# Placing a kernel's zero matmuls by a sliding sum of TensorE work, with stores in threads of their own

## The chip, the cores and the metric

The program runs on one core of a Trainium2 chip. The metric is the device time of the whole program in microseconds (us); lower is better. Five runs of the kernel before are given.

## The reference

Two layers read the same input x (2048 positions by 512 channels, bfloat16) and are mixed by a gate:

```
g = sigmoid((x * gate_w).sum(-1))            # one number per position
q, k, v = split(x @ wqkv)                    # 32 heads of 16 channels
p = softmax(q @ k.T * 16**-0.5)              # 2048 x 2048 for each head
a = (p @ v) @ wo
dt = exp(log_dt); P = exp(dt*(A_re + i A_im) * l)      # l = 0 .. 2047, 128 states per channel
K = sum over states of C * P * dt*B, real part         # 512 x 2048 taps
b = causal_convolution(x, K) + x * Dskip               # the reference does it by FFT
out = g * a + (1 - g) * b
```

The attention needs 32 x 2048 x 2048 exponentials, and nothing else in the program is as large. The convolution is done here by blocks: a table of powers, a state recurrence over 32 chunks of 64 positions, and small matmuls.

## The kernel before, in words

**A program planned ahead.** The Python code runs a planner. Each instruction is an object `O` with an engine, the buffers it reads and writes, a planned cost, and for a matmul a number of `u` units of TensorE work. `Prog.put` appends it to its engine's list, notes a planned end time, and derives the semaphore waits. Engines then run their lists strictly in order. What the planner gets wrong shows up as an engine that stands.

**The backbone.** Scores are made in slots of 128 keys by 512 queries; 2048 slots are grouped three to a tile, 683 tiles in all. For tile t, `fill` issues three score matmuls (operands Qm and KT) into one of two PSUM buffers SC0 and SC1, and `ex` (line 720) issues one ScalarE exponential over all three slots into a ring of SBUF buffers (ET, EX, EL, EM). A fill of tile t+2 must wait for the exponential of tile t. The loop over t at the end of `record` is this backbone.

**Relief for ScalarE.** From a certain tile on, `dchoose` may take one slot of a tile away from ScalarE. VectorE then makes its exponential: one instruction from PSUM (line 732), and for each pair of such slots four instructions into DP and DC (`dpoly`, lines 752, 847, 847, 756). The exponential of that tile covers 1024 columns and not 1536, and the slot's value matmul becomes three matmuls, of which one reads VC, a scaled copy of V made once by `vcopy` (line 795). The tuples `RINGS` and `DWS` say from which tile on which ring is used.

**Everything else is threads.** Value matmuls (`pv`, into PSUM OA), projections, the power table (`table`), the tap stage (`kstage`: Kst, stored to gm_kpd), the state stage (`sstage`: Sst, stored to gm_sd), the recurrence (`scan`), the output stage (`ystage`: Yst, stored to gm_ytd), the gate (64 one-column matmuls) and the output projection are Python generators with priorities; a lower number goes first. Each yields lists of instructions, or a condition: AFTER a mark, Q for a tile number, LOCK for the one spare PSUM bank MB. `Sched.run` picks, for each tile, what is ready by the plan. In the kernel before, a stage yields its own store to DRAM, so its store carries the stage's priority (table 9, kstage 8, ystage 7.5, sstage 7), and loads (`qload`, `sload`, `yload`, `yread`) have 6. All of these DMAs are issued from SyncE's queue (SP) in order. A DMA that transposes (Qt, SG, Yl) holds SP for several us while it is issued.

**Zero matmuls.** `keep` and `keepsc` make a 128x128x512 matmul with an all-zero weight tile `wm`. They add zero to OA, MB or SC and change nothing but TensorE's activity. Where they go is decided by a debt: each tile adds 2.3 units per us of exponential (`WARM`), each matmul pays its units, the debt is cut to between 0 and 4, and after the other work of a tile zero matmuls are added while more than .2 is owed:

```
sch.debt = max(0.0, min(4.0, sch.debt - sch.units)) + WARM * (e1 - e0)
...
while sch.debt - sch.units > .2 and p.free["PE"] + .3 < lim:
```

**Units.** A 128x128x512 matmul is 1 unit; a fill of three is 1; four value matmuls are 1; a gate matmul is set to .05, 3.2 for all 64.

Of the kernel before, what the change touches and what calls it, by code (L numbers as in the profile page):

```python
# [13 lines left out]
P = 128  # L14
# [16 lines left out]
NO = 14  # L31
RINGS = ((24, "ET", NE), (400, "EL", 11), (548, "EM", 14))
DWS = ((400, 548 - 4, "DPL", "DCL", 4, 4.6), (548, 9999, "DPM", "DCM", 7, 5.5))
WARM = 2.3
DEBT = 2.4
SOLO = 1.0
ORDER = """
B161^ zr fo OnTp1^ OnTp0 DPL MU^ Yl gp Py^ wm msk Tt VV D48^ Qp3^ SG2^ EX^ OnT2^ Wo^ ldt tt2^ D32^ DPM Dp hpi^ L8^ g an^ ft1^ PT0^
Dpb^ EM^ X22 ET dt^ nwi^ X23^ EL^ idb Wv Kst u1 u4^ G ea OT BreT^ VE^ pt1^ B160 OnT3 L1^ e2 Qp2^ OnT0 cb^ D16^ Qm L48^ BimT^ x0n^
SG0 PT1^ VC KT^ L16 u2^ ON^ Yst^ Q0 L32^ AreT u3^ Rz^ DCM X20 ge Q1 Q2 SG1 DCL CreT s2^ s3 zi^ FP^ Wk CimT Sst tt1^ pt2 ft2^ Q3  # L40
OnT1^ VL idf L4^ sb_^ X21 Wq gwT Qt bn wrb AimT^ piota^ xT sgn B163 L2 ba^ B162 g1
"""
# [40 lines left out]
class Prog:  # L83
# [4 lines left out]
    def __init__(self, bufs):  # L88
        self.bufs = bufs
        for b in bufs.values():  # L90
            b.st, b.tags, b.closed, b.first, b.last = {}, {}, False, None, None
        self.q = -1
        self.log = []
        self.ops = {e: [] for e in self.ENG}
        self.cnt = {e: 0 for e in self.ENG}
        self.known = {e: {} for e in self.ENG}
        self.snap = {}
        self.dn = [0] * NDSEM
        self.dnext = 0
        self.need = {e: set() for e in self.ENG}  # L100
        self.te = {}
        self.free = {e: 0.0 for e in self.ENG}
        self.aend = 0.0

    def _deps(self, eng, R, W):
# [85 lines left out]
    def put(self, o):  # L191
# [28 lines left out]
        else:  # L220
            self.free[eng] = t + o.c
            e = t + (o.c if o.l is None else o.l)
        self.te[(s, i)] = e
        self._record(eng, o.fn, deps, s, i, o.R, o.W)
        return e

    def emit(self, nc, es):
# [37 lines left out]
class Sched:  # L265


    def __init__(self, prog):
        self.p = prog
        self.thr = []  # L270
        self.flag = set()
        self.lock = {}
        self.n, self.units, self.debt = 0, 0.0, 0.0

# [42 lines left out]
    def emit(self, th):  # L317
        for o in th[3]:
            self.p.put(o)
            if o.eng == "PE":  # L320
                self.units += o.u
        self._next(th)
        self.control()
# [12 lines left out]
    def run(self, now, pe_end, dve_end, margin=.02):  # L336
        p = self.p
        self.control()
        while True:
            best = None  # L340
            holder = [t for t in self.thr if t in self.lock.values()]
            for th in holder + [t for t in self.thr if t not in holder]:
# [8 lines left out]
                if ops[0].dma:  # L351
                    if max(r, f) > pe_end:
                        continue
                    k = 0
                elif eng == "PE":
                    c = sum(o.c for o in ops)
                    if max(f, r) + c > pe_end or self.debt - self.units > DEBT and sum(o.u for o in ops) < 2.3 * c:
                        continue
                    k = 0 if r <= f + .03 else 2
                elif eng == "DVE":  # L360
                    if max(f, r) > dve_end:
                        continue
                    k = 0 if r <= f + .03 else 1 if r <= f + .16 else 2
                else:
                    if r > now:
                        continue
                    k = 0
# [180 lines left out]
def record(p, B, ins):  # L548
# [11 lines left out]
    def mm(out, lhsT, rhs, R, W, start=True, stop=True, pos=None, c=.22, l=.4, u=1.0):  # L560
        kw = {} if pos is None else dict(tile_position=pos)
        return O("PE", lambda t: t.matmul(out(), lhsT(), rhs(), start=start, stop=stop, skip_group_check=True, **kw), R, W, c, l, u)  # L562

    def dv(fn, R, W, n, k=1):
# [227 lines left out]
    def vcopy():  # L792
        yield ("Q", DWS[0][0] - 5)
        yield [dv(lambda v: v.memset(VC(272, [[288, 16], [1, 16]]), 0.0), [], [(VC, 1)], 256)]
        yield [dv(lambda v: v.tensor_scalar(VC(0, [[288, 16], [34, 8], [1, 34]]), VE(34, [[560, 16], [68, 8], [1, 34]]), C3, None, ALU.mult),
                  [(VE, c) for c in range(16)] + [(VE, "one"), (VE, "pad")], [(VC, 0)], 4352, 4)]

    def pv(q):
# [3 lines left out]
        for j in range(4):  # L802
# [8 lines left out]
            if isd:  # L811
# [4 lines left out]
                rounds[1].append(mm(out, ve, lambda DP=DP, o=o: DP(o, [[1, 512]]), rv + [(DP, k, g["n"])], [(OA, 0, b)], False, False, **kw))  # L816
                rounds[2].append(mm(out, vc, lambda DC=DC, o=o: DC(o, [[1, 512]]), [(VC, 0), (VC, 1), (DC, k, g["n"])], [(OA, 0, b)], False, kt == 15, **kw))
        os = [o for r in rounds for o in r]
# [174 lines left out]
    def table():  # L993
# [5 lines left out]
        for pb in range(NBLK // 2):  # L999
            qr, blks = pb // 2, (2 * pb, 2 * pb + 1)  # L1000
            PT = PTs[pb % 2]
            if pb > 1:
                yield ("AFTER", f"K{2 * pb - 3}")
            B16 = B[f"B16{qr}"]
# [17 lines left out]
            for i, blk in enumerate(blks):  # L1022
                yield [dma("SP", lambda e, i=i, blk=blk, PT=PT: e.dma_start(ptd.dram(blk * P * PTN, [[PTN, P], [1, PTN]]), PT(i * PTN, [[1, PTN]])),
                           [W[i]], [(ptd, blk)], 6.5, .5)]
                sch.mark(f"pt{blk}")
                if blk == 15:
                    sch.mark("sgfree")
                sch.add(qload(blk), 6)
                sch.add(kstage(blk), 8)

    X2 = [B[f"X2{k}"] for k in range(4)]
# [9 lines left out]
    def kstage(blk):  # L1041
# [4 lines left out]
        for part, wn in ((0, "wrb"), (1, "nwi")):  # L1046
# [7 lines left out]
        sch.unlock("MB")  # L1054
        yield [dma("SP", lambda e: e.dma_start(kpd.dram(blk * P * 8 * P, [[8 * P, P], [1, 8 * P]]), Kst(1024 * (blk % 2), [[1, 8 * P]])),
                   [(Kst, blk % 2, blk), (Kst, "z")], [(kpd, blk)], 4.5, .4)]
        sch.mark(f"K{blk}")
# [3 lines left out]
    def sstage(blk):  # L1061
        q0, qr, bl = (blk % 2) * PTN, blk // 4, blk % 4
        for bank in range(4):
            yield ("LOCK", "MB", [(Qt, blk % 2, blk)])
            os = []
            for pp in range(2):
                for j in range(4):
# [9 lines left out]
            sch.unlock("MB")  # L1077
            yield [dma("SP", lambda e, bank=bank: e.dma_start(sd.dram((CB * blk + 8 * bank) * 8192, [[256, P], [4 * 8192, 2], [1, 256]]),
                                                              Sst(512 * bank, [[256, 2], [1, 256]])), [(Sst, bank, (blk, bank))],
                       [(sd, (blk, bank))], 2.7, .45)]  # L1080
        sch.mark(f"S{blk}")
# [75 lines left out]
    def ystage():  # L1157
        def unit(u):
# [11 lines left out]
            for qq in range(2):  # L1170
# [9 lines left out]
                for q in (2 * qq, 2 * qq + 1):  # L1180
                    for ri in range(2):
# [9 lines left out]
            sch.unlock("MB")  # L1191
            yield [dma("SP", lambda e: e.dma_start(ytd.dram(16 * u * S, [[T, P], [4 * S, 4], [1, T]]), Yst(r2 * 256, [[64, 4], [1, 64]])),
                       [(Yst, r2, u)], [(ytd, u)], 3.3, .65)]
            if hf == 1:
# [208 lines left out]
    def pvs(t, limit):  # L1403
        nonlocal pvn, opened
        done_ = 0
        while pvn < NQ and done_ < 2:
# [39 lines left out]
            put(*os)  # L1446
            sch.units += sum(o.u for o in os)
            sch.mark(("pv", pvn))
# [10 lines left out]
    while tile(t + 1):  # L1459
# [4 lines left out]
        e1 = e0 + (512 * len(acols(t + 1)) / 1200 + EXP if tile(t + 1) else 0)  # L1464
        sch.debt = max(0.0, min(4.0, sch.debt - sch.units)) + WARM * (e1 - e0)
        sch.units = 0.0
        sch.control()
        if tile(t + 2):
# [13 lines left out]
            put(*fill(t + 2))  # L1482
            sch.units += 1
            if t + 2 in dsel:
# [11 lines left out]
        pvs(t, lim)  # L1496
        while sch.debt - sch.units > .2 and p.free["PE"] + .3 < lim:
            if opened:
# [11 lines left out]
            put(o)  # L1510
            sch.units += 1
    p.late, p.forced = late, forced[0]
# [58 lines left out]
```

## Time and profile before

| | |
|---|---|
| median of 5 runs | 895.15 us (890.76 to 898.02) |
| the profiled execution | 897.99 us |
| its span on the core | 896.2 us |
| mean granted TensorE clock | 0.965 |
| busy: ScalarE, VectorE, TensorE | 866.1, 826.6, 786.8 us |
| exponentials of 1536 columns | 532 (382 ET, 18 EX, 76 EL, 56 EM) |
| exponentials of 1024 columns | 151 (72 EL, 79 EM) |
| zero matmuls | 579 (531 into OA, 46 into SC, 2 into MB) |
| DMA, mean over the span | 108 GB/s |

The page lists busy time by engine; PE is TensorE's matmuls, PEld its weight loads, DVE VectorE, ACT ScalarE, POOL GpSimdE, and SP the queue from which SyncE issues DMAs. PEclk is the clock that TensorE was granted: 1.00 is full. A name with "SC<-Qm,KT" is a matmul that writes SC and reads Qm and KT. Times inside the span start at its first instruction.

### The profile page before, as it was taken

Reading aid. Unit: us, or ns where it says so; the run is one execution under the profiler, and the core shown is the slowest. Engines: PE = TensorE matmul, PEld = TensorE weight load, DVE = VectorE, ACT = ScalarE, POOL = GpSimd, SP = SyncE. Lnnn points to the kernel's source line nnn. Section 1 sums busy time; section 2 is a strip of 40 time slices with the busy share of each in tenths; the row PEclk is TensorE's granted clock in tenths of the full one; section 3 lists DMA queues with packets and bytes.
Section 4 is the critical chain, followed back from the end, with each engine's and each line's share of the span. In section 5 each row is a group of like instructions: output and inputs, shape, how many; then the busy total and the mean of one; then the engine's idle time right before and its main releaser. Section 6 shows DMA issues by size and latency. Waiting matters only on the chain.

```text
span 896.2 us, 18273 instructions
## 1 busy us (share of the span) xinstructions
PE 786.8 (88%) x7487; PEld 246.9 (28%) x7487; DVE 826.6 (92%) x1769; ACT 866.1 (97%) x693; POOL 9.0 (1%) x18
## 2 busy tenths in 40 slices
PE   7999999888888888888888999998899989898987
PEld 2222232222222222222233333342233322222222
DVE  7999999999867899999999987799999999999992
ACT  6999999999998999999999999799999999999996
POOL 2000000000000000000000000000000000000000
PEclk9999997999997999999999799599999999999999
DMA  9400010006797989969499688566214101000000
GB/s 205 119 1 1 1 49 0 1 1 174 230 217 226 263 283 252 197 136 187 88 206 169 172 185 164 143 141 136 76 41 119 22 19 35 20 1 1 2 1 24
DMA packets 228562, 96.48 MB, mean 108 GB/s; under 512 B 192000, under 2 KB 215168, under 8 KB 226432
## 3 DMA queue, kind: packets, MB, share of 16 engines
q1 hardware_dynamic: 227280, 94.54, 44.0%
q8 instruction: 59, 0.97, 0.5%
q10 hardware_dynamic: 1200, 0.79, 0.3%
q14 instruction: 23, 0.19, 0.1%
HBM read 30.02 MB, written 37.75 MB: 76 GB/s over the span
## 4 chain that ended last, share of the span: by engine, by line
ACT 42%; DVE 41%; PE 12%; issue 2%; DMA 2%; POOL 1%; DVEq 0%; ACTq 0%; SPq 0%; POOLq 0%
ACT ET L720 31%; DVE s L847 9%; ACT EM L720 5%; PE OA L562 5%; PE SC L562 4%; DVE EL L732 4%; DVE DCM L847 4%; DVE DCL L847 3%; ACT EL L720 3%; DVE EM L732 3%; DVE G L847 3%; PE MB L562 3%; ACT EX L720 3%; DVE Sst L1075 2%; DVE SG L1117 2%
## 5 line engine op out<-in xcount | busy, mean ns | idle before, releaser
L720 ACT ACTIVATE ET<-SC 128x1536 bf16<-128x1536 f32 x382 | 516.3, 1601 | 8.6 <-PE SC L562 8.3
L562 PE MATMUL SC<-Qm,KT 32*128 32x512 bf16 x2048 | 274.6, 395 | 82.9 <-ACT ET L720 48.3
L562 PE MATMUL OA<-wm 128*128 128x512 bf16 x531 | 180.6, 404 | 2.8 <-DVE OT L835 1.6
L720 ACT ACTIVATE EL<-SC 128x1536 bf16<-128x1536 f32 (+1 forms) x148 | 169.9, 1305 | 4.8 <-PE SC L562 4.1
L562 PEld LDWEIGHTS SC<-Qm,KT 32*128 32x128 bf16 x2048 | 67.8, 91 | 332.1 <-ACT ET L720 172.4
L720 ACT ACTIVATE EM<-SC 128x1024 bf16<-128x1024 f32 (+1 forms) x135 | 148.8, 1254 | 0.8 <-PE OA L562 0.4
L562 PE MATMUL OA<-ET,VE 128*32 128x512 bf16 x1146 | 117.6, 404 | 0.0
L847 DVE TENSOR_TENSOR s<-G,MU 128x256 f32<-128x256 f32 x240 | 92.5, 420 | 3.4
L847 DVE TENSOR_TENSOR tt<-B,D 128x1024 bf16<-128x1024 bf16 x96 | 62.7, 682 | 0.5
L562 PEld LDWEIGHTS OA<-wm 128*128 128x128 bf16 x531 | 39.0, 99 | 85.9 <-issue 76.1
L1075 DVE TENSOR_TENSOR Sst<-MB,sgn 128x512 bf16<-128x512 f32 x64 | 43.6, 681 | 13.1 <-PE MB L562 13.0
L732 DVE TENSOR_SCALAR EM<-SC 128x512 int16<-128x512 f32 x78 | 51.8, 677 | 0.0
L847 DVE TENSOR_TENSOR s<-s,SG 128x256 f32<-128x256 f32 x120 | 50.0, 417 | 0.0
L847 DVE TENSOR_TENSOR G<-s,s 128x256 f32<-128x256 f32 x120 | 49.8, 415 | 0.1
L732 DVE TENSOR_SCALAR EL<-SC 128x512 int16<-128x512 f32 x72 | 47.9, 679 | 0.5 <-PE SC L562 0.5
L562 PEld LDWEIGHTS OA<-ET,VE 128*32 128x32 bf16 x1146 | 29.2, 94 | 67.3 <-issue 65.9
L562 PE MATMUL OA<-EL,VE 128*32 128x512 bf16 x444 | 44.9, 399 | 0.6 <-DVE OT L835 0.6
L562 PE MATMUL OA<-EM,VE 128*32 128x512 bf16 x404 | 39.6, 388 | 0.1
L835 DVE STREAM_TRANSPOSE OT<-OA 128x512 f32<-128x512 f32 x32 | 22.7, 708 | 17.6 <-PE OA L562 17.6
L562 PE MATMUL MB<-Qt,X 64*32 64x256 bf16 x512 | 29.7, 308 | 10.0 <-DVE Sst L1075 7.8
L847 DVE TENSOR_TENSOR ft<-FP,L 128x1024 f32<-128x1024 f32 (+1 forms) x32 | 33.8, 1086 | 0.4
L1117 DVE CAST SG<-G 128x256 bf16<-128x256 f32 x120 | 34.1, 284 | 0.1
(163 smaller groups left out, 837.6 us busy)
## 6 DMA issues: line engine op xcount, KB each, us to landing
gm_ptd<-PT SPq DMA_DIRECT2D x16, 1024.0 KB, 6.2
Py<-gm_ptd SPq DMA_DIRECT2D x32, 512.0 KB, 4.6
gm_sd<-Sst SPq DMA_DIRECT2D x64, 128.0 KB, 2.6
gm_kpd<-Kst SPq DMA_DIRECT2D x16, 256.0 KB, 4.0
Tt<-gm_kpd SPq DMA_DIRECT2D x128, 32.0 KB, 3.7
gm_xrd<-in_A_x_dram SPq DMA_DIRECT2D x1, 2048.0 KB, 11.0
X<-gm_xrd SPq DMA_DIRECT2D x8, 256.0 KB, 5.0
gm_ytd<-Yst SPq DMA_DIRECT2D x32, 64.0 KB, 2.3
```

Of the source, the lines that this page charges most:

```text
L562: return O("PE", lambda t: t.matmul(out(), lhsT(), rhs(), start=start, stop=stop, skip_group_check=True, **kw), R, W, c, l, u)
L720: return ac(lambda a: a.activation(b(o, F), sc(0, F), AF.Exp, scale=LN2 / 128), [(sc, n, (t, n)) for n in ns], [et(t, n)[2] for n in ns], ...
L732: yield [dv(lambda v: v.tensor_scalar(b(o, [[1, 512]]).bitcast(I16), sc(512 * n, [[1, 512]]), -EOFF, EOFF, ALU.max, ALU.add), [(sc, n, (t, ...
L835: yield [dv(lambda v: v.transpose(OT(0, [[1, 512]]), OA(0, [[1, 512]])), [(OA, 0, b)], [(OT, 0, b)], 560)]
L847: return dv(lambda v: v.tensor_tensor(o(), a(), b_(), f), R, W, n, k)
L1075: yield [dv(lambda v, bank=bank: v.tensor_tensor(Sst(512 * bank, [[256, 2], [1, 256]]), MB(0, [[256, 2], [1, 256]]), sgn(0, [[0, 2], [1, 2 ...
L1117: return dv(lambda v: v.tensor_copy(sg(2 * RS * r, [[RS, 2], [1, 128]]), G(256 * (r % 2), V2)), [(G, r % 2)], [(sg, bl, (qr, 'G')) for bl ...
```

## The change

Four things change together.

1. The debt is gone. The planner keeps a history of TensorE's planned work, and `lack(t)` sums the units of the last 3.413 us before t. Zero matmuls are added while that sum is under 7.6 units, or the last half window under 3.34; other matmul groups are admitted only if the sum does not fall too far behind.
2. The stores of table, kstage, sstage and ystage (16, 16, 64 and 32 of them) become threads of their own with priority 5.9, just ahead of the loads. The stage goes on at once. The table's reuse of a PT buffer now names the taps and stores of both blocks of that buffer.
3. The scaled copy of V is made by four instructions, each for four key tiles, and a value matmul that needs VC reads only its own quarter.
4. Rings and relief windows start a little earlier (tile 380 and 540 for 400 and 548), and the SBUF places of the buffers (`ORDER`) are new.

```diff
-RINGS = ((24, "ET", NE), (400, "EL", 11), (548, "EM", 14))
-DWS = ((400, 548 - 4, "DPL", "DCL", 4, 4.6), (548, 9999, "DPM", "DCM", 7, 5.5))
-WARM = 2.3
-DEBT = 2.4
+RINGS = ((24, "ET", NE), (380, "EL", 11), (540, "EM", 14))
+DWS = ((380, 540 - 4, "DPL", "DCL", 4, 4.6), (540, 9999, "DPM", "DCM", 7, 5.5))
+NEED = 7.6
+WIN = 3.413
+HALF = .44
+TOL = .2
...
+        if eng == "PE":
+            self.hist.append((self.free[eng], o.u))
...
+    def lack(self, t):
+        v, u, h = 0.0, 0.0, NEED * HALF
+        for e, w in reversed(self.hist):
+            if e <= t - WIN:
+                break
+            if e > t - WIN / 2:
+                h -= w
+            u += w
+        return max(NEED - u, h)
...
-                    if max(f, r) + c > pe_end or self.debt - self.units > DEBT and sum(o.u for o in ops) < 2.3 * c:
+                    at = max(f, r) + c
+                    if at > pe_end or now < 1e8 and p.lack(pe_end) - sum(o.u for o in ops) > TOL + max(0, int((pe_end - at) / .24)):
                         continue
...
+    def spawn(op, pr, name=None):
+        def g():
+            yield [op]
+            if name:
+                sch.mark(name)
+        sch.add(g(), pr)
...
-        yield [dv(lambda v: v.tensor_scalar(VC(0, [[288, 16], [34, 8], [1, 34]]), VE(34, [[560, 16], [68, 8], [1, 34]]), C3, None, ALU.mult),
-                  [(VE, c) for c in range(16)] + [(VE, "one"), (VE, "pad")], [(VC, 0)], 4352, 4)]
+        for k in range(0, 16, 4):
+            yield [dv(lambda v, k=k: v.tensor_scalar(VC(288 * k, [[288, 4], [34, 8], [1, 34]]), VE(34 + 560 * k, [[560, 4], [68, 8], [1, 34]]),
+                                                     C3, None, ALU.mult),
+                      [(VE, c) for c in range(k, k + 4)] + [(VE, "one"), (VE, "pad")], [(VC, ("c", k // 4))], 1088, 4)]
...
-                yield ("AFTER", f"K{2 * pb - 3}")
+                for n in ("K", "pt"):
+                    for k in (4, 3):
+                        yield ("AFTER", f"{n}{2 * pb - k}")
...
-            yield [dma("SP", lambda e, bank=bank: e.dma_start(sd.dram((CB * blk + 8 * bank) * 8192, [[256, P], [4 * 8192, 2], [1, 256]]),
-                                                              Sst(512 * bank, [[256, 2], [1, 256]])), [(Sst, bank, (blk, bank))],
-                       [(sd, (blk, bank))], 2.7, .45)]
+            spawn(dma("SP", lambda e, bank=bank: e.dma_start(sd.dram((CB * blk + 8 * bank) * 8192, [[256, P], [4 * 8192, 2], [1, 256]]),
+                                                             Sst(512 * bank, [[256, 2], [1, 256]])), [(Sst, bank, (blk, bank))],
+                      [(sd, (blk, bank))], 2.7, .45), 5.9)
...
-        while sch.debt - sch.units > .2 and p.free["PE"] + .3 < lim:
+        while p.lack(lim) > 0 and p.free["PE"] + .3 < lim:
```

The other three stores change as the one of Sst does, and the remaining lines of the debt are removed.

## The prediction

> **What bounds the kernel now.** I read the engine totals and the clock row of the page first.
>
> ```profile
> PE 786.8 (88%) x7487; PEld 246.9 (28%) x7487; DVE 826.6 (92%) x1769; ACT 866.1 (97%) x693; POOL 9.0 (1%) x18
> ...
> PEclk9999997999997999999999799599999999999999
> ```
>
> ScalarE (ACT) is the bound, and five dents in the clock row (slices of 22.4 us) say where it may lose time. In the list of exponentials the distance from one end to the next has a median of 1.343 us for 1536 columns and 0.917 us for 1024. So the profiled time splits up: first tile done 15.83, then 531 x 1.343 + 151 x 0.917 = 851.6, distances longer than those medians 20.06, last exponential to the span's end 8.70, outside the span 1.80; sum 897.99 us. Only the 851.6 and the 20.06 can move.
>
> Next, the busy time by stretch. The clock record puts the half-clock stretches at 130.4 to 144.0, 277.1 to 287.4, 372.7 to 376.1, 495.6 to 505.8 and 557.0 to 580.9: 13.65, 10.24, 3.41, 10.24 and 23.89 us, or 4, 3, 1, 3 and 7 times 3.413 us. Here are those stretches, each after the 3.4 us ahead of it:
>
> ```profile
> core 0: us, PE busy (x) PEld busy (x) DVE busy (x) ACT busy (x) POOL busy (x), PEclk, DMA share, GB/s
> 126.90:130.40 3.50, 3.06 (x51) 1.45 (x48) 3.50 (x8) 3.50 (x4) 0.00 (x0) 0.99 0.00 0
> 130.40:144.00 13.60, 13.44 (x76) 3.04 (x76) 12.72 (x23) 11.77 (x11) 0.00 (x0) 0.50 0.00 1
> 273.70:277.10 3.40, 2.05 (x17) 0.51 (x16) 1.41 (x4) 3.40 (x4) 0.00 (x0) 1.00 1.03 413
> 277.10:287.40 10.30, 10.13 (x61) 2.29 (x61) 9.34 (x18) 8.10 (x6) 0.00 (x0) 0.50 0.46 170
> 369.30:372.70 3.40, 2.05 (x28) 0.83 (x27) 3.37 (x10) 3.40 (x4) 0.00 (x0) 1.00 1.11 298
> 492.20:495.60 3.40, 2.61 (x66) 1.54 (x62) 3.37 (x11) 3.40 (x4) 0.00 (x0) 1.00 0.89 268
> 553.60:557.00 3.40, 2.10 (x47) 1.06 (x46) 3.37 (x12) 3.40 (x3) 0.00 (x0) 1.00 0.71 150
> 557.00:580.90 23.90, 23.90 (x285) 7.79 (x284) 18.49 (x54) 18.25 (x14) 0.00 (x0) 0.50 0.59 140
> ```
>
> See in it: ACT, full ahead of each stretch, falls to 18.25 of 23.90 inside it. Of the 20.06 us, 15.8 lie in the five stretches (2.5, 2.9, 0.8, 2.6, 7.0) and 4.2 elsewhere. I then weighed each matmul by the array it uses (rows x columns x streamed columns over 128 x 128 x 512) and summed by 3.413 us windows in step with the clock record: the windows just ahead of the five stretches hold 4.56, 5.50, 4.50, 4.75 and 3.50 units, and the lowest full-clock window that nothing follows holds 5.12. So a weak window of about 5 units costs clock. Why they are weak, the waits say:
>
> ```profile
> PE MB L562 <- DVE Sst L1075: 11.0, 20, 1.3
> ACT ET L720 <- PE SC L562: 8.3, 17, 0.9
> PE MB L562 <- DVE Yst L1190: 2.8, 4, 1.3
> ```
>
> In four of the five TensorE stood in order for up to 1.3 us on the MB bank; the first (126.9) holds the gate's one-column matmuls, which the plan counts at 3.2 units and which weigh 0.125.
>
> **Zero matmuls.** By the instruction order they go from 579 to 625: 46 more, x 0.21 us (two take 0.61, three 0.82) = 9.7 us of TensorE, which had 109 us free. In a tile with a full MB they can push a fill and so ACT; I take 0, bound 1 us, since ACT's whole wait for fills at full clock was part of the 4.2. What they buy is where they stand. I laid both programs' matmuls along their exponentials at 1.343 and 0.917 us: the time in which the last 3.413 us hold under 5.0 units falls from 9.4 to 1.6 us, under 5.5 from 23.9 to 14.8. Between tiles 85 and 450 (120 to 620 us) nothing under 5.0 is left, where it was 8.5 us; after 620 us it grows from 0.9 to 1.6. Five episodes scaled by 1.6/9.4 are 0.85, by 14.8/23.9 are 3.1; as the windows that fired lay at 3.5 to 5.5, I take 2. At 15.8/5 = 3.2 us each that leaves 6.4 of 15.8: gain 9.4, bounds 5.9 and 13.1.
>
> A row against this: those windows had PE busy for 2.05 to 3.06 us of 3.4, its longest wait was 1.30 us, and the clock still fell. The Trainium skill, "TensorE: Matmul & The Clock Gate", section "HAM oscillation", has as its rule that idle gaps over some 3.4 us are what costs clock. By that rule no zero matmul was needed and this part gains 0 (894.6 in the sum below); this trace disagrees. The same page (section "What's actually happening") wants one busy window for full clock again, while 557.0 to 580.9 was busy for 23.90 of 23.90 us and stayed at half for seven.
>
> **Relief moved.** The order shows 524 exponentials of 1536 and 159 of 1024 (before 532 and 151): 523 x 1.343 + 159 x 0.917 = 848.2, a gain of 3.4 us on the path. For it VectorE gets 8 x (0.68 + half of 0.41 + 0.68 + 0.68 + 0.41) = 14.2 us more, and TensorE 16 more value matmuls (0.1 us or less each in their column groups). Cover for the 14.2: VectorE stands for 18.9 us between 224 and 314 and 13.2 between 515 and 582, but is full late:
>
> ```profile
> 224.00:314.00 90.00, 75.50 (x673) 21.45 (x677) 71.09 (x131) 87.59 (x66) 0.00 (x0) 0.94 0.90 234
> 515.00:582.40 67.40, 63.28 (x885) 24.54 (x881) 54.16 (x159) 61.75 (x46) 0.00 (x0) 0.82 0.76 164
> 604.80:873.60 268.80, 243.52 (x2285) 74.47 (x2289) 267.29 (x547) 267.31 (x246) 0.00 (x0) 1.00 0.16 39
> ```
>
> So the eight cost nothing if earlier work of VectorE moves up into the 32 us, and up to 14.2 if not.
>
> **Stores.** SP issues 390 DMAs in both. A transposing load of Qt holds SP for 5.4 us (median); a store ready at the same moment now passes it, and the load is 0.45 us later. The trace shows what a late store does: at 275.7 VectorE ended a 2.51 us wait of the Kst cast for an earlier gm_kpd store, and TensorE then stood 1.07 us on MB, which opened the second episode. In the changed order the last Sst comes at tile 312 and not 376, the last recurrence step at 409 and not 427, the last Yst at 495 and not 521: at some 0.68 us or less per instruction this is work that leaves the late, full part of VectorE, so the 14.2 are covered. The mark that the table now awaits adds no instruction; queued behind it are a block pair's 14 VectorE instructions (9 us), whose stores gate Qt. I take 0 for this part alone, bounds -2 (the 2.5 us wait gone) and +3 (two such waits anew).
>
> **V's copy.** One instruction of 1.23 us becomes four; the nearest row (128 x 1024, 16-bit, 0.42 us) gives 1.7: 0.5 us more VectorE at tile 375, 0 on the path. New SBUF places: 10 more waits on VectorE, 4 on TensorE, of some 1,100 each: 0.
>
> **Sum.** 897.99 - 3.4 - 9.4 = 885.2 for the profiled execution. It lies 2.84 above the median, about one episode; scaling the median's loss in the same ratio (15.8 - 2.84 = 13.0, of which two fifths stay) gives 895.15 - 3.4 - 7.8 = 884.0. I say 884. With no episode it is 878.8, and 877 if 1.8 of the 4.2 go too.
>
> **Rivals.** First, the episodes come back: four of five began with an in-order wait that the plan did not foresee, and VectorE is planned fuller between tiles 120 and 240, so waits on MB can be as many. For it: the 20 waits for Sst. Against it: a stand of 1.3 us takes about 3 units, and there is now more around it. Time 890 to 894.6 (897.99 - 3.4). Second, slower: the transfers jam. DMA share was 0.85 between 201.6 and 320 and 0.78 to 440. The same ptd, kpd, Qt and sd traffic ran over tiles 141 to 376 and now over 141 to 312; 0.82 x 235/171 = 1.13. If 1 were the ceiling, 0.13 x 171 x 1.343 = 30 us of delay would fall on 16 blocks, 1.9 us each, on TensorE in front of its Qt matmuls; stands of 1.05 and 1.30 us cost ACT 0.72 and 0.85, so 0.65 x 30 = 20 us: 897.99 - 3.4 + 20 = 914, half of it 904. It decides from the point where Qt lands later than the plan's 12 us; it landed in 7.6 to 9.9. Against it: single 6.4 us stretches show shares of 1.2. Third, the eight slots find VectorE full: 885.2 + 14.2 = 899 at most.
>
> **How the numbers follow.** Forecast 0.64 (877 to 889); episodes back 0.22 (889 to 896, a third of it under 890.7); VectorE full 0.05 (892 to 899); jam 0.09 (over 900). The measurement can tell about 0.5% from no change: 890.7 to 899.6. Faster 0.64 + 0.07 and a little of the rest = 0.73, same 0.18, slower 0.09. The range 877 to 895 leaves out the jam, the worst of the third, and the lowest edge.
>
> **What would show it.** Exponentials 524 and 159, distances 1.343 and 0.917; two half-clock stretches or fewer between 120 and 620 us, the likeliest near 130 us (the gate) or after 800; ACT's distance loss 10 to 11 us for 20.06; VectorE's idle time between 224 and 314 under 10 us; last Yst before 700 us. Wrong, if five stretches are there again, if Qt lands after 12 us, or if waits of ACT for line 732's tiles appear late.

## The result and the profile after

The changed kernel takes 902.37 us (median of 23 runs, 897.3 to 908.7), the kernel before 894.9 us (44 runs, 888.87 to 902.18). The ratio is 1.008, interval 1.0057 to 1.0103: slower, where 884.0 and faster were forecast. (Runs of either kernel spread by 1.3 to 1.5%. The profiled one of the kernel after, 898.45 us, lies low in its spread and the one of before, 897.99 us, high, so the two profiles differ by less than the medians.)

The engine totals and the clock row of the page, after:

```profile
PE 786.0 (88%) x7549; PEld 247.8 (28%) x7549; DVE 839.1 (94%) x1796; ACT 860.9 (96%) x693; POOL 9.2 (1%) x18
...
PEclk9999999999997899999999999999999999999999
```

ScalarE (ACT) has 5 us less work, of which eight wide exponentials turned narrow explain 8 x (1.343 - 0.917) = 3.4, and still the span is not shorter. The clock row has one dip, in the slices from 269 to 314 us, where before it had four spread over the kernel (slices from 134, 269, 493 and 560 us; the fifth half-clock stretch, 3.41 us at 372.7, is too short to show there). The clock record gives six half-clock stretches between 120 and 620 us, at 273.0, 286.6, 317.3, 351.5, 450.5 and 525.6 us, 34.1 us in all (before 61.4). Split up as in the prediction, the profiled execution is: first tile done 14.18, nominal distances 848.2 (524 exponentials of 1536 columns, 159 of 1024), distances longer than nominal 25.58, then 8.70 and 1.80. Of the 25.58 us, 19.7 lie between 245 and 400 us, where before there were 3.8.

Busy time by stretch, after: first the two longest half-clock stretches, then two of the stretches that the prediction used.

```profile
core 0: us, PE busy (x) PEld busy (x) DVE busy (x) ACT busy (x) POOL busy (x), PEclk, DMA share, GB/s
273.00:279.80 6.80, 6.77 (x44) 1.56 (x44) 6.11 (x12) 4.18 (x3) 0.00 (x0) 0.50 1.14 251
286.60:300.30 13.70, 7.85 (x52) 1.58 (x55) 6.79 (x12) 5.84 (x5) 0.00 (x0) 0.50 0.98 278
...
224.00:314.00 90.00, 70.14 (x649) 20.68 (x645) 73.76 (x132) 76.56 (x58) 0.00 (x0) 0.89 0.99 256
...
604.80:873.60 268.80, 236.75 (x2210) 71.08 (x2207) 264.32 (x534) 267.92 (x247) 0.00 (x0) 1.00 0.13 33
```

Between 286.6 and 300.3 TensorE, VectorE and ScalarE are all half idle: they wait for something that is none of them. Over 224 to 314 ScalarE has 76.56 us of work where it had 87.59, and the DMA share is 0.99 where it was 0.90. After 604.8 ScalarE is busy for 267.92 of 268.80 us. The waits, after:

```profile
PEld MB L576 <- DVE Sst L1099: 28.4, 29, 6.4
...
PE MB L576 <- DVE Sst L1099: 21.9, 20, 5.8
...
ACT ET L741 <- PE SC L576: 20.2, 17, 6.1
...
DVE Sst L1099 <- DMA gm_sd<-Sst: 15.7, 6, 5.9
```

(Sum in us, number, longest.) The last row is new (the waits of before have none of Sst for a store): VectorE, about to write an Sst slot, waits for the store that empties it. The timeline around the longest of these waits shows the whole chain (start, length, engine and line, tile; in brackets the idle time ahead and what ended it; SPq is SyncE's queue):

```profile
284.45 1.05 SPq L1048 DMA_DIRECT2D gm_ptd<-PT  x2
...
285.55 2.44 SPq L1102 DMA_DIRECT2D gm_sd<-Sst  x2
...
288.03 7.50 SPq L1061 DMA_TRANSPOSE Qt<-gm_ptd  x1
292.78 0.69 DVE L1099 TENSOR_TENSOR Sst<-MB,sgn 128x512 bf16<-128x512 f32 x1 [5.87 <-DMA gm_sd<-Sst]
...
293.53 0.65 PE L576 MATMUL MB<-Qt,X 64*32 64x256 bf16 x8 [5.85 <-DVE Sst L1099]
...
294.77 1.45 ACT L741 ACTIVATE ET<-SC 128x1536 bf16<-128x1536 f32 x1 [6.14 <-PE SC L576]
```

Two 1 MB stores of the table go out, then two 128 KB stores of Sst. By the DMA records the four land at 289.01, 291.65, 292.76 and 293.40: the small ones need 7.2 and 6.7 us, where the plan allows 2.7. VectorE stands 5.87 us in front of the Sst write, TensorE 5.85 us in front of the next MB matmul, and since the score matmuls are queued behind that, ScalarE stands 6.14 us.

### The profile page after: what moved, and what is told of

The parts are those of the page before. It is cut to its first block, busy times and chain, and to the rows that moved or that the text cites. A ratio compares the mean times of both kernels' runs of the same rounds, so it can differ in the third digit from the quotient of the medians.

```text
span 896.7 us, 18426 instructions
## 1 busy us (share of the span) xinstructions
PE 786.0 (88%) x7549; PEld 247.8 (28%) x7549; DVE 839.1 (94%) x1796; ACT 860.9 (96%) x693; POOL 9.2 (1%) x18
## 4 chain that ended last, share of the span: by engine, by line
DVE 52%; ACT 37%; DMA 5%; PE 3%; issue 3%; SPq 0%; ACTq 0%; DVEq 0%
ACT ET L741 13%; ACT EL L741 13%; DVE s L870 9%; ACT EM L741 8%; DVE tt L870 4%; DVE Sst L1099 4%; DMA gm_sd<-Sst 4%; DVE EM L753 3%; DVE G L870 3%; DVE DCM L870 3%; DVE ft L870 3%; ACT EX L741 3%; DVE EL L753 3%; DVE DCL L870 3%; DVE PT L870 2%
## 5 line engine op out<-in xcount | busy, mean ns | idle before, releaser
L741 ACT ACTIVATE ET<-SC 128x1536 bf16<-128x1536 f32 x362 | 489.4, 1624 | 20.6 <-PE SC L576 20.2
L576 PE MATMUL SC<-Qm,KT 32*128 32x512 bf16 x2048 | 270.5, 389 | 70.0 <-ACT ET L741 23.4
L576 PE MATMUL OA<-wm 128*128 128x512 bf16 x582 | 185.8, 394 | 3.1 <-DVE OT L858 2.0
L741 ACT ACTIVATE EL<-SC 128x1536 bf16<-128x1536 f32 (+1 forms) x160 | 184.8, 1366 | 0.1
L741 ACT ACTIVATE EM<-SC 128x1024 bf16<-128x1024 f32 (+1 forms) x143 | 155.9, 1268 | 0.8 <-PE SC L576 0.5
L576 PE MATMUL OA<-ET,VE 128*32 128x512 bf16 x1086 | 109.8, 399 | 0.4 <-DVE OT L858 0.4
L1099 DVE TENSOR_TENSOR Sst<-MB,sgn 128x512 bf16<-128x512 f32 x64 | 43.6, 681 | 16.6 <-DMA gm_sd<-Sst 15.7
L753 DVE TENSOR_SCALAR EM<-SC 128x512 int16<-128x512 f32 x86 | 56.8, 679 | 0.1
L576 PE MATMUL OA<-EL,VE 128*32 128x512 bf16 x480 | 47.2, 389 | 0.2 <-DVE OT L858 0.2
L576 PE MATMUL OA<-EM,VE 128*32 128x512 bf16 x428 | 41.6, 388 | 0.1
```

The lines of the kernel that those rows point to most:

```text
L741: return ac(lambda a: a.activation(b(o, F), sc(0, F), AF.Exp, scale=LN2 / 128), [(sc, n, (t, n)) for n in ns], [et(t, n)[2] for n in ns], ...
L753: yield [dv(lambda v: v.tensor_scalar(b(o, [[1, 512]]).bitcast(I16), sc(512 * n, [[1, 512]]), -EOFF, EOFF, ALU.max, ALU.add), [(sc, n, (t, ...
L1099: yield [dv(lambda v, bank=bank: v.tensor_tensor(Sst(512 * bank, [[256, 2], [1, 256]]), MB(0, [[256, 2], [1, 256]]), sgn(0, [[0, 2], [1, 2 ...
```

## The experiments

The letters in the expectations stand for theories. A and B in e1 and e2 are explained there; from e3 on, A: Sst has too few slots. C: the DMA engines are over-full. D: SyncE's queue is. E: the order of the instructions is bad in itself. F: a late small store costs only where its slot is written again. G: the wait moves on. Any other is explained where it stands. "Loss" is the sum of the distances over nominal, as above. Each ratio is to the kernel before on the same chip. A kernel that is planned anew also gets SBUF places of its own; e5, e9 and e13 keep those of the changed kernel, e10 those of e1.

**The parts.** e1 is the kernel before with `lack`, its calls and no debt. e2 is the kernel before with the four `spawn` stores and the table's marks.

```diff
 # e1, and the other lines of the debt
-        while sch.debt - sch.units > .2 and p.free["PE"] + .3 < lim:
+        while p.lack(lim) > 0 and p.free["PE"] + .3 < lim:
 # e2, and the same for gm_ptd, gm_kpd, gm_ytd
-            yield [dma("SP", ... sd.dram(...), 2.7, .45)]
+            spawn(dma("SP", ... sd.dram(...), 2.7, .45), 5.9)
```

> The kernel before with the new placing of zero matmuls alone (682 of them for 579; stores, V copy and rings as before). Theory A (the stores, issued earlier, press the transfers and Sst waits for them): last Sst stays at tile 375, no jam between 250 and 320 us, fewer half-clock stretches (3 or fewer), exponentials' distance loss 20 falls to about 10 us; the plan relieves 144 slots for 151, +3 us; time 5 to 8 us under the kernel before, about 888. Theory B (the admission rule and the extra zero matmuls hold up the fills): slower than before by 4 to 8 us, as the whole change is.

> The kernel before with the stores in threads of their own alone (debt, V copy, rings as before). Theory A: last Sst at tile 307, DMA share about 1.06 between 250 and 320 us, Sst waits for gm_sd for 10 us or more, exponentials lose 12 us or more between 250 and 320 us; total 6 to 12 us over the kernel before. Theory B: the stores cost nothing; time within 0.5% of before or 3 us under it (158 slots relieved for 151).

e1: 885.37 us (881.64 to 890.28), ratio 0.9896 (0.986 to 0.9932). e2: 909.15 us (904.4 to 912.99), ratio 1.0164 (1.0122 to 1.0206). The stores alone make the kernel slower than before, in e2 by 15 us and not the 6 to 12 expected; the long wait there is that of Kst for gm_kpd (up to 9.5 us), while Sst waited for gm_sd for 2.3 us in all and not for 10. In e1 the loss is 3.5 us, with no half-clock stretch before the end, and ScalarE never stands where the changed kernel does (busy time by stretch, e1):

```profile
245.00:270.00 25.00, 21.56 (x192) 6.16 (x191) 15.33 (x30) 25.00 (x20) 0.00 (x0) 1.00 1.04 207
270.00:295.00 25.00, 21.38 (x198) 6.33 (x198) 21.27 (x40) 25.00 (x20) 0.00 (x0) 1.00 0.98 288
295.00:320.00 25.00, 21.44 (x207) 6.73 (x211) 24.90 (x49) 25.00 (x20) 0.00 (x0) 1.00 0.90 236
```

e7 adds V's copy in four to e1. e8 adds only the gm_ptd stores, e14 only the gm_kpd stores, e15 all four kinds; e15 is the changed kernel without the ring borders and V's copy:

```diff
 # e8, on e1 (e14: the same for gm_kpd<-Kst)
-                yield [dma("SP", ... ptd.dram(blk * P * PTN, ...)]
-                sch.mark(f"pt{blk}")
+                spawn(dma("SP", ... ptd.dram(blk * P * PTN, ...), 5.9, f"pt{blk}")
```

> The new rule for zero matmuls alone (the kernel of 885.4 us in the first series) with V's scaled copy in four parts added, and nothing else. The prediction took this part at 0: 883 to 888 us. If the four parts cost three more VectorE instructions' overhead on a critical place, or the order that follows is worse, over 890.

> The new rule for zero matmuls alone, and of the stores only the 16 gm_ptd ones queued apart from their stage; the 64 gm_sd, 16 gm_kpd and 32 gm_ytd stores stay in their stages. The state stage keeps nearly its pace (first, middle and last Sst block at tiles 158, 250 and 371; in the changed kernel 158, 234 and 312; with the zero-matmul rule alone 158, 262 and 375). Theories C and D both: what jams is the denser state stage, not stores queued apart as such, so 883 to 889 us. If any store queued apart brings the jam, by reaching SyncE in another order: over 893.

> The zero-matmul rule, and of the stores only the 16 gm_kpd ones queued apart. First, middle and last Sst block at tiles 158, 260 and 380, as with the rule alone (158, 262, 375). If what costs is the denser state stage: 882 to 888 us, loss under 8. If any store queued apart costs, by being planned nearer to the next write of its slot: 890 or more, with a wait of Kst on gm_kpd of over 3 us.

> The changed kernel without the new ring borders (400 and 548 again) and without V's copy in four parts: the zero-matmul rule and all four kinds of stores queued apart. The state stage runs at the changed kernel's pace (158, 234, 312). If the stores alone make the loss: 898 to 906 us, loss 20 or more, waits on gm_sd or gm_kpd or Qt over 5 us. If the ring borders or V's copy have a share: under 894.

e7: 887.86 us, ratio 0.9883 (0.9837 to 0.9929), not to be told from e1: V's copy costs nothing that this measurement can show. e14: 887.82, 0.9952 (0.9927 to 0.9978). It lost nothing between 245 and 400 us, and no wait of Kst on gm_kpd appeared; but its whole loss was 11.2 us and not under 8, of which 3.6 us lie near 140 and 3.7 between 420 and 460 us, in and behind half-clock stretches at 130.0, 423.6 and 440.7. e8: 894.06, 0.9974 (0.9946 to 1.0002), with 9.7 us lost between 245 and 400: just on the side of the second expectation. Its first half did not keep the pace that was expected, though: the 33rd Sst write came after 93 tiles, where e1 has 106. e15: 901.71, 1.0111 (1.0071 to 1.0152), its loss 28.9 and its wait for gm_sd up to 5.8: the ring borders and V's copy have no visible share.

**More slots, and a later landing in the plan.** e3 gives Sst eight slots at the same instruction order; e4 tells the planner that a gm_sd store lands after 8.0 us.

```diff
 # e3; slot bank becomes slot 4 * (blk % 2) + bank
-    sb("Sst", 4 * 512)
+    sb("Sst", 8 * 512)
 # e4
-                      [(sd, (blk, bank))], 2.7, .45), 5.9)
+                      [(sd, (blk, bank))], 8.0, .45), 5.9)
```

> The changed kernel with eight Sst slots for four, so that a slot's next write comes a whole block later; same instructions in the same order on every engine. Theory A (Sst waits for its own store's landing, and VectorE, MB, TensorE and ScalarE stand behind it): the wait of Sst for gm_sd goes from 15.7 us to under 2, the loss of the exponentials between 250 and 320 us from 17 to under 6, time about 885 to 888. Theory C (the DMA engines themselves are full, the wait only moves on): another wait (Qt, Kst or PT for a DMA) takes its place, loss in that stretch stays over 12 us, time 898 or more.

> The changed kernel, but the plan is told that a gm_sd store lands after 8.0 us and not 2.7 (the longest of the trace was 8.0); four slots as in the changed kernel. Theory A: the plan puts Sst where its slot is free, so VectorE does other work meanwhile; wait of Sst for gm_sd under 4 us, time 886 to 890, with the transfers as dense as in the changed kernel (last Sst at tile 302). Theory C: the jam stays, 898 or more.

e3: 904.66 us, ratio 1.0114 (1.0079 to 1.0148). e4: 900.66, 1.0075 (1.0046 to 1.0104). Theory A falls. In e4 Sst still waits for gm_sd (8.1 us in three waits, where under 4 was expected). In e3 that wait is gone and others are there (waits of e3):

```profile
DVE Kst L1075 <- DMA gm_kpd<-Kst: 8.4, 1, 8.4
PE MB L577 <- DMA Qt<-gm_ptd: 8.4, 4, 3.2
```

**Another queue.** e5 issues the gm_sd and gm_kpd stores from GpSimd's queue, e13 the gm_ptd stores; everything else keeps its order:

```diff
 # e5 (e13: ('ptd',))
+        for _, o in log:
+            if o.dma and o.W[0][0].name in ('sd', 'kpd'):
+                o.eng = "POOL"
```

> The changed kernel with the instruction order of TensorE, ScalarE and VectorE untouched, but with the gm_sd and gm_kpd stores (64 and 16 of them) issued on GpSimd's queue, so that they no longer stand behind the Qt transposing loads, which hold SyncE for 5.7 to 6.1 us each. Theory D (the issue queue of SyncE is over-full between 245 and 320 us: SyncE was issuing for 180 of the 220 us between 200 and 420 in the changed kernel, 148 in the one before): the waits 'DVE Sst <- DMA gm_sd<-Sst' (15.7 us) and 'DVE Kst <- DMA gm_kpd' vanish or fall under 3 us, the loss of the exponentials falls from 25.6 to under 10 us, and the time is 881 to 889. Theory C (the 16 DMA engines themselves are full: share 1.06 in that stretch): the stores land as late as before, the waits stay over 8 us, and the time stays at 897 to 905.

> The changed kernel with the instruction order of TensorE, ScalarE and VectorE untouched, and the 16 gm_ptd stores of 1 MB issued on GpSimd's queue instead of SyncE's; the small stores stay on SyncE's. In the changed kernel 22 of 80 gm_sd and gm_kpd stores landed after more than 5 us, 17 of them issued within 5 us behind a gm_ptd store of the same queue. If it is the order of the queue: hardly any of them lands after 5 us, no wait on gm_sd or gm_kpd over 2 us, loss under 14 us instead of 25.6, 882 to 890 us. If it is the DMA engines themselves, shared by all queues: 15 or more still land after 5 us, and Qt, whose load must wait for gm_ptd, lands later too, 895 to 906 us.

e5: 900.9 us, ratio 1.0049 (1.0016 to 1.0083). e13: 913.08, 1.0224 (1.0186 to 1.0262). Both miss what a pure queue theory asks, and e13 is slower than either of its expectations. (In both, 2.5 and 1.7 us come from the end, where 11.17 and 10.40 us follow the last exponential and not 8.70.) In e5 no wait on gm_sd or gm_kpd is left, but Qt lands after 10.5 us (median) and up to 17.0, and TensorE stands for it. Timeline of e5; the Qt loads now hold SyncE for up to 12.0 us each:

```profile
286.54 17.09 SPq L1070 DMA_TRANSPOSE Qt<-gm_ptd  x2
...
302.55 0.65 PE L585 MATMUL MB<-Qt,X 64*32 64x256 bf16 x8 [4.25 <-DMA Qt<-gm_ptd]
```

In e13, 15 of 80 small stores, alone with the loads on SyncE's queue, still landed after more than 5 us, Qt took up to 13.9, and Sst waited as before (waits of e13):

```profile
DVE Sst L1108 <- DMA gm_sd<-Sst: 14.7, 8, 3.9
```

So what is short seems to lie behind the queues. Not shown is how much GpSimd's queue adds of its own (its gm_sd stores landed after 5.1 us in the median, 3.5 in the changed kernel); no run issued the stores from a third queue. By the Trainium skill ("DMA: Bandwidth & Descriptors", section "Issuing engines are not separate DMA queues"), transfers share the same 16 DMA engines, whichever engine issues them. The 15 late stores of e13 agree with it.

**Less and more traffic at the same order.** e9 leaves out the transposition of Qt (so a part of the state computation): the load is then 128 packets of 8 KB and not 4096 of 256 B. e10 is e1 plus 64 useless stores from GpSimd's queue; in the trace they went as packets of 6 KB at 292 ns, 1.17 us of the 16 engines each.

```diff
 # e9
-e.dma_start_transpose(Qt((blk % 2) * PTN, [[128, 32], [1, 128]]), ptd.dram(...))
+e.dma_start(Qt((blk % 2) * PTN, [[1, PTN]]), ptd.dram(...))
 # e10, after each gm_sd store
+prog.put(O("POOL", lambda e, k=k: e.dma_start(X.dram(k * P * 1536, [[1536, P], [1, 1536]]), VE(0, [[1, 1536]])), ...
```

> The changed kernel with its instruction order kept on every engine, but the 16 Qt loads read 8 KB rows as they lie and leave out the transposition (so this kernel leaves out a part of the state computation: Qt holds the table untransposed). In the profile of the changed kernel a block's Qt load is 4096 packets of 256 B at 21.6 ns, that is 5.5 us of all 16 DMA engines; as 128 packets of 8 KB at 324 ns it is 2.6 us. Theory C (the 16 DMA engines are over-full: a block's transfers take about 13.4 us of them and the changed kernel plans a block in 10.0 tiles of 1.343, that is 13.4 us): the waits on gm_sd, gm_kpd and Qt vanish, the exponentials lose under 8 us instead of 25.6, 876 to 886 us. Theory E (not the volume, but the places in which state work now stands before score matmuls): the loss stays over 15, 888 to 900 us.

> The kernel with the zero-matmul rule alone (885.4 us in the first series, loss 3.5 us) with its order kept on every engine, plus 64 useless stores from GpSimd's queue, one after each gm_sd store has landed: 128 rows of 3 KB of a tile that is not written any more, to memory of their own. By the rows between 2 and 4 KB (84 and about 170 ns a packet) one takes about 1.0 us of the 16 DMA engines, a block's four 4 us. Its blocks are then about as full as those of the changed kernel (13.4 + 4 of 17.6 us, against 13.4 of 13.4). Nothing is added to SyncE. Theory C: Qt loads hold SyncE longer than 6.5 us on average and land late, the loss rises to 8 to 25 us, 889 to 905. Theory E, and a pure queue theory: no wait is added, 882 to 888 us.

e10: 930.18 us, ratio 1.0408 (1.0363 to 1.0453): traffic alone turns the fastest kernel into the slowest, more than expected, with no instruction of TensorE, VectorE, ScalarE or SyncE moved. Qt took 12.2 us (median) and up to 20.6. Waits of e10:

```profile
ACT ET L754 <- PE SC L589: 33.7, 23, 6.3
...
DVE Sst L1109 <- DMA gm_sd<-Sst: 13.3, 4, 6.8
...
DVE G L1148 <- DMA SG<-gm_sd: 8.8, 3, 5.6
...
PE MB L589 <- DMA Qt<-gm_ptd: 7.3, 2, 4.1
```

e9: 893.09, ratio 0.9998 (0.9961 to 1.0035); the loss fell from 25.6 to 15.5, not to under 8, and both figures lie in the range that its expectation gave to E. Small stores were late as often as in the changed kernel (27 of 80 after more than 5 us, there 22), and 5.6 us of the loss follow one wait for gm_sd that ends at 287 us (waits of e9):

```profile
DVE Sst L1099 <- DMA gm_sd<-Sst: 7.9, 2, 5.8
```

So fewer packets took away 10 us and left the rest. Against E as the whole cause stands e10, where nothing but traffic was added and the loss rose from 3.5 to 46.2. C held in direction in both, and in size in neither.

**The pace.** e6 raises the planner's figures for SyncE's transfers. e11 keeps them and adds one condition to `qload`; e12 is e11 with eight Sst and four Kst slots; e16 and e17 are e11 with other numbers.

```diff
 # e11, in qload, under `if blk >= 2:`
+            yield ("Q", 144 + 13 * blk)
 # e16 (e17: 9 for 12)
+            yield ("Q", 144 + 15 * min(blk, 7) + 12 * max(0, blk - 7))
 # e6: Qt holds 6.3, SG 7.0/3.2, gm_kpd 5.5/.8, and
-                      [(sd, (blk, bank))], 2.7, .45), 5.9)
+                      [(sd, (blk, bank))], 4.5, .85), 5.9)
```

> The changed kernel with the planner's figures for SyncE raised to what the trace measures: a Qt load holds the queue 6.3 us (was 5.6), an SG load 3.2 (2.6), a gm_sd store .85 (.45) and lands after 4.5 (2.7), a gm_kpd store .8 (.4) and lands after 5.5 (4.5). The planner then slows the state stage by itself: the middle Sst block comes at tile 242 instead of 234. Theory D (the queue of SyncE): SyncE's share of issuing between 245 and 320 us falls below .9, the loss falls under 12 us, 884 to 891 us. Theory C (the DMA engines): the traffic is nearly as dense, share 1.0 or over, so the waits go to Qt and SG landings, and the time is 893 to 901.

> The whole change, all stores still queued apart, with one line more: the Qt load of block b is not planned before tile 144 + 13 b, so that a block has 13 tiles (17.5 us) as in the kernel before, instead of 10. First, middle and last Sst at tiles 158, 250 and 354 (changed kernel 158, 234, 312). Theory C: share of the DMA engines between 245 and 320 us under 1.0, Qt lands within 11 us, no wait on gm_sd or gm_kpd over 2 us, loss under 8 us, 880 to 888 us. Theory E: the loss stays over 15 us, 890 to 900.

> The whole change, paced as in e11 (the Qt load of block b not before tile 144 + 13 b), with Sst in 8 slots instead of 4 and Kst in 4 instead of 2, so that a store that lands late holds up no write. In e11 9 us of the 22 that the exponentials lose lie at 298 us, behind one wait of 6.9 us of a Kst write on its gm_kpd store. Theory F (late small stores cost time only where their slot is written again): no wait on gm_sd or gm_kpd is left, the loss falls from 22 to 9 to 14 us, 880 to 888 us. Theory G (the wait moves on, to Qt or SG landings, as it did when Sst alone got 8 slots): loss 17 or more, 890 to 897 us.

> The whole change, all stores queued apart, with the Qt load of block b not planned before tile 144 + 15 b for blocks 0 to 7, then 12 tiles more for each block. First, 32nd and last Sst write at tiles 158, 264 and 362 (kernel before 157, 260, 376; changed kernel 158, 234, 312). If the pace of the blocks is the cause: the exponentials lose under 4 us between 245 and 400 us (changed kernel 19.7, paced at 92 tiles 9.4), and the time is 881 to 889 us. If stores queued apart cost by themselves: 8 us or more there, 890 to 897.

> As e16, but after block 7 each block follows 9 tiles later: 158, 264 and 338, so the second half takes 74 tiles for eight blocks, 12.4 us a block, less than the 13.9 us that its transfers take of the 16 DMA engines. If the pace is the cause: under 4 us lost between 245 and 360 us, and a loss of 6 to 15 us between 360 and 470, 886 to 896 us. If not the pace but something in the first half (the table's stores, which end there) makes the loss: none in the second half either, 880 to 887.

e6: 892.1 us, ratio 0.9957 (0.9926 to 0.9988), between its two expectations, with one wait of 8.5 us of the recurrence for an SG load. e11: 895.47, 1.0025 (0.9994 to 1.0056). e12: 893.49, 0.9999 (0.9973 to 1.0024). e11 misses what C asked, and e12 falls on the side of G, so F falls: each still has one wait of 7 us, and with more slots it only changed its place, from Kst on gm_kpd (6.94 us) to the recurrence. From the waits of e12:

```profile
DVE G L1140 <- DMA SG<-gm_sd: 7.1, 1, 7.1
```

e16: 883.46 us (881.42 to 888.92), ratio 0.9905 (0.9874 to 0.9937). e17: 885.06, 0.992 (0.9892 to 0.9947). With the first half at its old pace, the whole change is as fast as e1. In e17 the second half takes 71 tiles by the trace (changed kernel 76). It loses 1.2 us between 360 and 470 us and 4.2 between 450 and 500, less than the 6 to 15 expected if pace as such were the cause, and its time lies in the range of the other expectation: what costs lies in the first half, where the table's stores are. Busy time of e16 in the stretch shown for the changed kernel, 224 to 314 us, with ScalarE full and the clock whole:

```profile
224.00:314.00 90.00, 78.22 (x729) 23.38 (x726) 89.14 (x165) 90.00 (x68) 0.00 (x0) 1.00 0.90 269
```

**One measure for all of them.** The packet records of the changed kernel between 215 and 430 us give a mean price by size: 22.2 ns for 256 B, 31 for 512 B, 100 for 2 KB, 324 for 8 KB, 13 for 128 B. Over 16 engines a Qt load of 4096 packets is then 5.7 us, an SG load 2.8, a gm_ptd store 2.6, an X load 1.7, a gm_kpd store 0.8 and a gm_sd store 0.5. The order of each kernel tells how many it issues between its first and its 33rd Sst write. In the changed kernel these are 8 Qt, 4 SG, 12 gm_ptd, 4 X, 9 gm_kpd and 32 gm_sd: 118 us of transfers in 77 tiles x 1.343 = 103 us, that is 1.14. Such ratios are an estimate from these rows: in e9 and e10 the mean of 256 B is 23.4 and 26.8 ns. The trace bears this one out: the packets that started between the two writes took 114 us of 16 engines, and the stretch lasted 123 us, 20 more than its tiles at 1.343. Beside the ratios the measured loss:

| kernel | tiles, first to 33rd Sst write | transfers to time | loss 245 to 400 us | whole loss |
|---|---|---|---|---|
| e16, e17 | 113, 109 | 0.83, 0.84 | 1.3, 1.1 | 6.3, 8.2 |
| e7 | 108 (trace) | 0.89 | 0.2 | 7.3 |
| e9 (its Qt load 2.6 us) | 77 | 0.90 | 11.1 | 15.5 |
| e1, e14 | 106, 105 | 0.91, 0.92 | 0.3, 0.0 | 3.5, 11.2 |
| before | 104 | 0.93 | 3.8 | 20.1 |
| e11, e12 | 100 | 0.94 | 9.4, 8.6 | 22.4, 21.3 |
| e6 | 86 | 1.00 | 8.0 | 15.4 |
| e8 | 93 | 1.03 | 9.7 | 15.5 |
| e2, e4 | 77, 74 (traces) | 1.09, 1.13 | 19.5, 15.9 | 35.1, 31.1 |
| after, e15, e3 | 77 | 1.14 | 19.7, 21.9, 21.9 | 25.6, 28.9, 28.0 |
| e5, e13 (small or table stores from GpSimd) | 77 | 1.14 | 13.3, 25.4 | 25.3, 34.5 |
| e10 (its 32 stores of 1.17 us included) | 106 | 1.17 | 22.7 | 46.2 |

In the second half the table's stores are gone. In the changed kernel's trace all packets that started between the 33rd and the last Sst write took 100.7 us of 105.4, in e17 87.2 of 97.5. That would explain why a dense second half is cheap; no run tests it alone.

Between 0.90 and 0.94 the measure does not decide: e1 and e14 lie there with nothing lost, before with 4 us, and e9, e11 and e12 with 9 to 11. In these three most of it follows one wait, and each time the late store was issued right behind two table stores: gm_sd at 279.50 us in e9 landed after 7.6 us, gm_kpd at 294.47 in e11 after 7.3, gm_kpd at 297.60 in e12 after 8.7, with the SG load behind it. Such pairs are in e1 and in the kernel before as well; why they cost nothing there is open.

## Why the prediction was wrong

**The step that failed: the stores, "I take 0 for this part alone", with bounds of -2 and +3.** They cost 18 to 19 us: 0.0197 x 895 from e7 (0.9883) to the changed kernel (1.008), 0.0215 x 895 from e1 to e15. Without the new zero matmuls they cost 15 (e2). The prediction priced them by one 0.45 us shift of a Qt load and one 2.51 us wait for a store, counted as at most two such waits. What the stage became was in the same paragraph: "the last Sst comes at tile 312 and not 376". That was booked as VectorE work moved forward, a credit; it was the debit, because eight Sst blocks and twelve table stores then had 77 tiles instead of 104. With the same stores and the old pace of the first half (e16) the cost is gone.

**The rival that was right had the wrong trigger and 0.09.** "The transfers jam" worked out 0.82 x 235/171 = 1.13 over the stage; the measure above gives 1.14 for its first half. That the two agree is chance: they are for different stretches and from different rows. Its 20 us on ScalarE compare with 19.7 measured between 245 and 400 us, 15.9 more than before. But it was to decide only "from the point where Qt lands later than the plan's 12 us", and Qt landed after at most 11.4. What came late was the small stores (22 of 80 after more than 5 us, before 10 of 80; 17 of the 22 were issued within 5 us behind a gm_ptd store), which the plan takes to land after 2.7 and 4.5 us. Single short stretches of share 1.2 were no argument against it: by 25 us from 245 to 320 the changed kernel has 1.06, 1.06 and 1.06, the kernel before 1.08, 0.82 and 1.00, and e1 1.04, 0.98 and 0.90, so that only the longer stretch tells them apart. And its 914, and half-way 904, left out the gain of the zero matmuls; with it, the same working gives 905.

**Zero matmuls, gain 9.4 (5.9 to 13.1): the number held, partly by luck.** e1's ratio is 0.0104 under 1, 9.3 us of 895, interval 6.1 to 12.5. Its parts were not as forecast: it has 682 zero matmuls and not the 625 that were counted, no half-clock stretch was left instead of two (e7's profiled execution has one, at 472.4 us), and the loss fell by 16.6 us between the two profiled executions, while the nominal time rose by 2.6 (538 and 145 exponentials). The dents that the prediction counted as five in the clock row are four; its five stretches stand in the clock record. The Trainium skill's rule in "TensorE: Matmul & The Clock Gate", section "HAM oscillation", that idle gaps over some 3.4 us are what costs clock, would have made this gain 0; e1 speaks against it. The changed kernel does not show its case either: its one stand of TensorE over 3.4 us (5.85, from 287.7) began inside a half-clock stretch that had started at 286.6, and the gaps just ahead of the falls at 273.0, 286.6 and 317.3 us were 2.4, 2.5 and 2.9 us.

**Relief moved, gain 3.4: the count held** (524 and 159, 848.2 us), and its cover too, as ScalarE has 267.92 of 268.80 us after 604.8. But it comes from the stores: without them there are 145 short exponentials, with them, unpaced, 159 to 161 (e2, e15). They give 6 us of nominal time and take 22 of loss.

**V's copy and new places at 0: nothing seen against it** (e7; e15, which has other places than the changed kernel). **Signs named in advance:** the last Yst at 681.6 (under 700) was right; wrong were two half-clock stretches or fewer (six), a loss of 10 to 11 us (25.58), and VectorE idle for under 10 us between 224 and 314 (16.2). Of the signs for "wrong", as many half-clock stretches as before came (six for five); Qt after 12 us, on which the jam was to be told, never showed.

**What stays open.** Why e9, e11 and e12 lose one stand of 6 to 7 us that e1 and the kernel before escape, and how much each store kind adds inside the jam; no run queues the gm_sd stores alone apart. No version beats e1 clearly: e16 (0.9905) and e1 (0.9896) are the same by this measurement, both faster than the kernel before and than the changed one.

## What to carry to other kernels

When a change lets a stage run ahead, sum that stage's transfers at their packet prices over the new, shorter stretch, half by half, before booking the earlier finish as a gain. In this kernel a half at 0.83 or 0.84 lost about 1 us and every half at 1.00 or more lost 8 to 25 (between 245 and 400 us); near 0.9 single transfers decided. A store that empties a slot is a dependency like a load: behind two megabytes it landed after 7 us and not 2.7, the writer waited in order, and everything queued behind waited too. Another slot or another queue only moved such a wait (e3, e5, e12); the old pace in the first half removed it (e16, e17), and fewer packets took away a part (e9).

## What the runs showed of the hardware

- A transposing load of 1 MB takes 4096 packets of 256 B at 18 ns (median) to 22 ns (mean), and it holds the issuing queue about as long as its packets take: 5.7 us on average in e1 and 5.8 in the changed kernel, 7.3 in e5 and 7.4 in e10 where another queue shared the engines, 0.8 as a plain load in e9.
- In the changed kernel small stores landed in the order of issue behind large ones: 128 KB behind 2 x 1 MB in 7.2 us, where the median of e1 is 2.5. On GpSimd's queue (e5) the median landing was 5.1 us.
- A weak window does not always cost clock. Weighed by 3.413 us windows as in the prediction, windows of 2.75 (at 269.6 us), 3.25 (283.2) and 3.25 units (313.9) of the changed kernel were followed by two, four and one half-clock windows; in e1 windows of 4.00 (660.4) and 4.75 units (762.8) were followed by none, and its clock was whole from 5.0 to 878.8 us. In the changed kernel itself a window of 4.75 units (682.6) was followed by none and one of 5.25 (447.1) by one. The prediction's "about 5 units" is no threshold.
- The end of the first exponential lies at 15.5 to 15.9 us or at 13.8 to 14.3 us. e5, e9 and e13, with the order and places of the changed kernel, have 15.8 to 15.9 where it has 14.18: 1.7 us between profiled executions that the change does not explain.
